# Two 14-megabyte streams of weights on another DMA queue, a conversion step in another order, and the second part's sums formed inside the last group of the first

## The chip, the cores and the metric

The kernel runs on one core of a Trainium2 chip. Its time is the device time of one execution, in microseconds (us). TensorE (PE in the profile) multiplies, VectorE (DVE), ScalarE (ACT) and GpSimd (POOL) do elementwise work, and SyncE (SP) issues nearly all DMAs of the kernel before. A DMA is an instruction in an engine's own stream: it stands in order between that engine's other instructions, waits there for its own condition, and what is behind it waits with it.

## What is computed

Three independent results in fp32, all of them from one launch:

```python
# attention: B, H, S, D = 4, 8, 576, 64, with a memory read mixed in
# moe:  x (2304, 512), w_in (512, 2048), w_out (2048, 512)
h = x @ w_in
g = np.maximum(0.01 * h, h)
moe = g @ w_out
# moe2: x (2304, 512), w_a and w_b (512, 1536), w_out (1536, 512)
a = x @ w_a
b = x @ w_b
moe2 = a * b @ w_out
```

Attention is untouched by the change and ends near 195 us. What follows is about moe and moe2.

## The kernel before, in words

**Every operand is a pair.** An fp32 matrix is held as a high and a low copy of a type that TensorE takes at full rate, and one product is three matmuls (`three`, lines 393 to 396: L394 and L395 need the high copy of the moving operand, L396 its low copy). A high copy is a cast, usually on ACT (L1064, L1326, L1177); the low copy is a subtraction on DVE or POOL one slot later (L1065, L1328, L1182).

**moe** goes over the 2304 tokens in part 0 (1024 tokens) and part 1 (1280), and over eight groups of 256 hidden columns. `inward` makes a group's hidden values: matmuls with `w`, the leaky ReLU on ACT (L1100, into `gf`), the cast on ACT (L1064, into tiles called `qs`, `hl`, `xs`, `g`) and the subtraction (L1065). `outward` multiplies them with `w_out` and adds to `xf` on DVE (L1118). Group 0 is done first for both parts (195 to 241 us); then part 0 runs the sets of groups [1,2], [3,4], [5,6], [7] (241 to 397 us), and part 1 runs [1,2] (397 to 461), [3,4] (461 to 523), [5] (523 to 566) and [6,7] (566 to 622).

**The weights are converted while this runs.** Raw weights come as pairs of 32-bit words (L178, `wraw`). An item of 128x512 is converted in four quarters, one after another on DVE: `one` (L292, L293), `two` (L304, L305), `three_` (L311), `four`; ACT makes the absolute value that an item begins with, here called the sign step (`absolute`, L261, into `wh`), and the high copy (`high`, L299 for moe's own weights into `w`, L301 for the last items into `wr`). Before, the quarter `two` of item n also issues `high` of n and the sign step of item n+1. There are three kinds of items: moe's own (`four` is L316 and L317), 24 "plain" ones of w_a and w_b (`four` is L324) and 12 "last" ones of moe2's w_out (`four` is L334 and L335). `convert(w, rate)` after each slot issues quarters in proportion to the slot's width. The scratch tiles `wh`, `wa`, `wr` exist twice, so item n+2 writes over those of item n.

**Where weights go.** A finished group of moe is written to `kept` in DRAM (L320, 14 times 1 MB) and read again for part 1 (L367, 14 times 1 MB). Plain items go to `plain` (L331), last items to `saved` (L337 from `wr`, L338 from `wh`). All of these are issued by SP, in the order of the program, and so is the next `wraw`.

**moe2** uses a seven-product scheme for w_a and w_b. It needs sums of the token matrix (S1 to S4, made by DVE at L1173, cast by L1178 or L1177, low copies by L1184 on DVE or L1182 on POOL) and sums of the weights (`Matrices.make`, one of 12 pairs after another). In pr 0 it runs over the tokens of part 0 (622 to about 808 us), in pr 1 over the rest. A block q is a string of products, by their digits, and of output slots O, which multiply the last finished a*b (tiles `hl`, `qs`; cast L1326, low copy L1328) with w_out: before, the string of an odd q is `1O6O5OO7234`, that of an even one `1657O2O3O4O`. Products are taken out of PSUM by L1343 and joined by L1370, all on DVE, as the slots of O are (L1405). At the end of pr 0 come the O slots of the last group, O(5,0) first, and there, from the slot (O, 5, 2) on, before forms the second part's sums, with two jobs per slot, while its last outputs run.

**What sets the order.** Code is written in the order of the slots; `after(k, fn)` puts a piece of work k slots later and `tick` runs what is due. An engine then executes its own instructions strictly in that order. There is no dynamic scheduling.

Of the kernel before, what the change touches and what calls it, by code (L numbers as in the profile page):

```python
# [117 lines left out]
def attention_moe_moe2(ctx: ExitStack, tc, kqT, qn, vn, m_prev, beta, w_in, w_out, w_a, w_b, w_o2, out):  # L118
# [38 lines left out]
    class Weights:  # L157


        def __init__(self, first, ab, last):  # L160
# [6 lines left out]
            self.plain = [dram.tile([P, 4, 2 * P], F32, tag=f"plain{m}", name=f"plain{m}") for m in range(12)]  # L167
# [116 lines left out]
        def quarters(self, n, item):  # L284
# [29 lines left out]
            def four():  # L314
                if kind == "own":
                    V.tensor_tensor(t["a"], t["a"], f32(self.tiles[i][:, 0, c]), ALU.subtract)  # L316
                    V.tensor_tensor(self.tiles[i][:, 1, c], t["a"], t["h"], ALU.add)  # L317
                    if part:
                        w = f32(self.tiles[i]).rearrange("p s c -> p (s c)")
                        nc.sync.dma_start(self.kept[i], w)  # L320
                    self.done.add(item)
                elif kind == "plain":
# [6 lines left out]
                    v = t["r"].rearrange("p (f c) -> p f c", f=2)  # L329
                    for f in range(2):  # L330
                        nc.sync.dma_start(self.plain[i][:, (0, 3, 1, 2)[part * 2 + f]], v[:, f])  # L331
                    self.done.add(item)
                else:
                    V.tensor_tensor(t["a"], t["a"], t["r"], ALU.subtract)  # L334
                    V.tensor_tensor(t["h"].bitcast(F32R), t["a"], t["h"], ALU.add)  # L335
# [795 lines left out]
    class Sums:  # L1131
# [27 lines left out]
        def jobs(self, y, raw):  # L1159
# [9 lines left out]
            def of(x, k):  # L1169
                return plain(x)[:, k] if x[0] == "A" else raw[(int(x[1]) - 1) * 2 + k]  # L1170
# [9 lines left out]
            def lo(x, eng):  # L1180
# [6 lines left out]
            early = [[hi("A11"), lo("A11", G)]]  # L1187
            middle = [
                [total("S1", "A21", "A22", ALU.add)],
                [total("S2", "S1", "A11", ALU.subtract), hi("S1")],  # L1190
                [hi("S2"), lo("S2", V)],
                [lo("S1", V), total("S4", "A12", "S2", ALU.subtract)],
                [hi("A12"), lo("A12", G), total("S3", "A11", "A21", ALU.subtract)],
                [hi("S3"), lo("S3", V)],
            ]
            end = [[hi("S4"), lo("S4", V)], [hi("A22"), lo("A22", G)]]
# [402 lines left out]
```

## Time and profile before

| | us |
|---|---|
| median of 3 runs | 1049.18 (1048.68 to 1051.09) |
| profiled execution | 1049.15 |
| its span | 1047.4 |
| PE busy | 1007.4 (96%) |
| DVE busy | 797.4 (76%) |
| ACT busy | 416.6 (40%) |
| POOL busy | 337.2 (32%) |

The execution is 1.8 us longer than its span. PE is busy nearly all the time, so that the question is what it loses in which stretch: where it stands still, and where the granted clock is at its lower level afterwards. The views are the table of stretches (busy time of each engine, the granted clock as a share of the full 2.4 GHz), the list of waits, and the instructions in order of time. A matmul's record is longer than the distance to the next one, because matmuls are pipelined.

### The profile page before, as it was taken

What the parts mean: (1) busy time and instruction counts of PE and PEld (TensorE: products, weight loads), DVE (VectorE), ACT (ScalarE), POOL (GpSimd) and SP (SyncE); (2) the same over time, 40 slices, a digit from 0 to 9 for tenths busy, and PEclk for the clock granted to TensorE, in tenths of its full rate; (3) what the DMA queues carried; (4) which work ended last, traced back from release to release, by engine and by line L of the source; (5) the groups of instructions that cost most, each with busy time, mean ns of one, the idle gap of its engine ahead of it and who ended that gap; (6) DMA issues with size and microseconds to landing.
All of it is one profiled execution on the core that took longest, in us unless ns stands there. A gap on an engine that the chain in (4) does not pass through costs nothing.

```text
span 1047.4 us, 14692 instructions
## 1 busy us (share of the span) xinstructions
PE 1007.4 (96%) x5266; PEld 806.4 (77%) x5266; DVE 797.4 (76%) x1555; ACT 416.6 (40%) x935; POOL 337.2 (32%) x324
## 2 busy tenths in 40 slices
PE   9999999989999999899979999999999999999998
PEld 4666667768878787687757888887777788888887
DVE  7999998789999987897976277677777736547546
ACT  7988885655353432315241523421222222101101
POOL 6787767312030311204011545544534100000000
PEclk9999999989999999899988999999999999999999
DMA  8325431255454578665774135666464433333412
GB/s 246 103 103 156 155 102 47 74 207 200 162 200 174 182 249 321 215 219 191 239 241 141 62 132 191 239 241 225 166 250 173 154 142 137 143 139 121 158 44 101
DMA packets 52729, 176.60 MB, mean 169 GB/s; under 512 B 5552, under 2 KB 18608, under 8 KB 42672
## 3 DMA queue, kind: packets, MB, share of 16 engines
q1 hardware_dynamic: 52512, 175.66, 48.2%
q8 instruction: 41, 0.67, 0.3%
q14 instruction: 32, 0.26, 0.1%
q10 hardware_dynamic: 144, 0.00, 0.0%
HBM read 117.44 MB, written 58.20 MB: 168 GB/s over the span
## 4 chain that ended last, share of the span: by engine, by line
PE 55%; DVE 28%; DMA 8%; ACT 4%; issue 3%; POOL 1%; SPq 0%; ACTq 0%; DVEq 0%; POOLq 0%
PE b L396 14%; PE b L394 14%; PE b L395 14%; PE b L745 4%; DVE wa L304 4%; PE b L824 3%; DVE xf L1118 3%; DVE wh L311 3%; DVE wh L292 3%; PE b L686 3%; DMA saved<-wh 2%; DMA wraw<-in_w_a 2%; DVE wh L305 2%; DVE wa L293 2%; DVE w L317 2%
## 5 line engine op out<-in xcount | busy, mean ns | idle before, releaser
L1343 DVE TENSOR_TENSOR gf<-b,gf 128x512 f32<-128x512 f32 x168 | 115.3, 688 | 76.2 <-PE b L396 72.5
L1405 DVE TENSOR_TENSOR xf<-b,xf 128x512 f32<-128x512 f32 (+1 forms) x91 | 62.1, 683 | 63.5 <-PE b L396 63.4
L394 PE MATMUL b<-xh,w 128*128 128x512 f32 x256 | 101.6, 397 | 0.4 <-ACT gf L1100 0.4
L395 PE MATMUL b<-xh,w 128*128 128x512 f32 x256 | 100.2, 391 | 0.0
L396 PE MATMUL b<-xh,w 128*128 128x512 f32 x256 | 99.9, 390 | 0.0
L1065 POOL TENSOR_TENSOR hl<-gf,hl 128x512 fp32r<-128x512 f32 (+1 forms) x26 | 36.7, 1422 | 168.1 <-ACT hl L1064 134.3
L261 ACT ACTIVATE wh<-wraw 128x512 f32<-128x512 f32 x64 | 43.0, 671 | 105.3 <-DMA wraw<-in_w_a 35.3
L395 PE MATMUL b<-xs,bhi 128*128 128x512 f32 (+1 forms) x216 | 79.7, 369 | 1.9 <-DVE xs L1184 1.9
L394 PE MATMUL b<-xs,bhi 128*128 128x512 f32 (+1 forms) x216 | 79.8, 369 | 0.6 <-DVE gf L1343 0.6
L396 PE MATMUL b<-xs,blo 128*128 128x512 f32 (+1 forms) x216 | 79.7, 369 | 0.0
L395 PE MATMUL b<-xs,ahi 128*128 128x512 f32 (+1 forms) x216 | 79.0, 366 | 0.0
L394 PE MATMUL b<-xs,ahi 128*128 128x512 f32 (+1 forms) x216 | 79.0, 366 | 0.0
L396 PE MATMUL b<-xs,alo 128*128 128x512 f32 (+1 forms) x216 | 78.9, 365 | 0.0
L640 ACT ACTIVATE p<-p,stat 128x512 f32<-128x512 f32 (+3 forms) x128 | 71.0, 559 | 4.5 <-DVE stat L694 4.2
L394 PE MATMUL b<-hl,w 128*128 128x512 f32 (+1 forms) x164 | 62.4, 380 | 10.1 <-ACT hl L1064 10.1
L1065 POOL TENSOR_TENSOR qs<-gf,qs 128x512 fp32r<-128x512 f32 (+1 forms) x21 | 30.3, 1451 | 124.2 <-ACT qs L1064 107.9
L667 POOL TENSOR_SCALAR p<-p,stat,keep 128x128 f32<-128x128 f32 (+3 forms) x95 | 61.4, 661 | 15.7 <-DVE stat L655 13.3
L395 PE MATMUL b<-hl,w 128*128 128x512 f32 (+1 forms) x164 | 62.2, 379 | 0.6 <-DVE hl L1065 0.6
L396 PE MATMUL b<-hl,w 128*128 128x512 f32 (+1 forms) x164 | 61.6, 376 | 0.0
L694 DVE CUSTOM_DVE_ANT_0 p<-b,mask 128x512 f32<-128x512 f32 (+3 forms) x128 | 57.6, 478 | 5.4 <-PE b L686 5.0
L1326 ACT CAST hl<-gf 128x512 fp32r<-128x512 f32 (+1 forms) x40 | 23.1, 578 | 96.3 <-DVE gf L1370 92.9
L396 PE MATMUL b<-w,hl 128*128 128x512 f32 (+1 forms) x146 | 57.5, 394 | 2.7 <-POOL hl L1328 1.4
(196 smaller groups left out, 2673.9 us busy)
## 6 DMA issues: line engine op xcount, KB each, us to landing
kept<-w SPq DMA_DIRECT2D x14, 1024.0 KB, 4.8
w<-kept SPq DMA_DIRECT2D x14, 1024.0 KB, 7.2
w<-saved SPq DMA_DIRECT2D x12, 1024.0 KB, 6.9
wraw<-in_w_in SPq DMA_DIRECT2D x16, 512.0 KB, 3.7
wraw<-in_w_out SPq DMA_DIRECT2D x16, 512.0 KB, 3.6
qraw<-in_qn SPq DMA_DIRECT2D x8, 768.0 KB, 6.7
wraw<-in_w_b SPq DMA_DIRECT2D x12, 512.0 KB, 4.3
plain<-wr SPq DMA_DIRECT2D x48, 128.0 KB, 4.0
```

The source lines that it names most:

```text
L261: nc.scalar.activation(t["h"], self.raw[n][:, :, 1].bitcast(F32), AF.Abs)
L304: V.scalar_tensor_tensor(u["a"], raw[:, :, 1], 0xC0000000, u["a"], ALU.bitwise_and, ALU.bitwise_or)
L394: nc.tensor.matmul(outp, l_hi, r_hi, start=start, stop=False)
L395: nc.tensor.matmul(outp, l_hi, r_lo, start=False, stop=False)
L396: nc.tensor.matmul(outp, l_lo, r_hi, start=False, stop=stop)
L640: nc.scalar.activation(t, t, AF.Exp, bias=s[:, 0, col : col + 1], scale=-1.0, accum_out=s[:, 1, col : col + 1])
L667: ENG[eng].tensor_scalar(live[p], live[p], stats[w % 3][:, 3, col : col + 1], k, ALU.mult, ALU.mult)
L694: nc.vector.tensor_tensor_reduce(one(p, [P, wd]), plan.tiles[banks[j]][:, c : c + wd], mask[:, off : off + wd], -0.125, BIG, ALU.add, ALU. ...
L745: nc.tensor.transpose(tt[0:kw, n * 128 : n * 128 + 128], live[name][:, kt * 128 : kt * 128 + kw], ident)
L1065: after(1 if eng is nc.vector else 2, lambda: eng.tensor_tensor(t[:, 1, c], gf, f32(t)[:, 0, c], ALU.subtract))
L1343: nc.vector.tensor_tensor(left[q, to], src, left[q, add], ALU.add)
L1405: nc.vector.tensor_tensor(y[:, i, c], op, y[:, i, c], ALU.add)
```

## The change

1. `kept` is written (L320) and read (L367) by DMAs that ACT issues instead of SP, each two slots later than before (`after(2, ...)`). That is 28 DMAs of 1 MB.
2. A plain item is written with one DMA instead of two; the sums of the weights read it through another layout (`PLACE`).
3. `high` of item n moves from quarter `two` to `three_`, the sign step of item n+1 from `two` to `four`. For the last items the second word of the pair is formed in `wa` instead of `wh` and saved from there.
4. The rates of `convert` fall from 0.7 to 0.4 in group 0's outward of part 0 (205 us) and from 0.85 to 0.75 in its inward of part 1.
5. moe2's strings become `16572O3O4OO` for an even q, and `1O65O7234OO` for the last block of pr 0; pr 1 has `16572O3O4OOOOTT`. The first O of a block thus stands one product later.
6. In `Matrices.make` the high and low copies, the next load and the write of the finished matrices are each one slot later.
7. The second part's sums are formed in the last block of pr 0 (q = 11), product by product (`1a`, `b6`, `5`, `cd7`, `2`, `3`, `4`), with their intermediate sums in the raw tile of the weights, and one job per slot.

```diff
-                nc.sync.dma_start(self.saved[i][:, 1, part], t["h"])
+                nc.sync.dma_start(self.saved[i][:, 1, part], t["a"])
...
-                        nc.sync.dma_start(self.kept[i], w)
+                        after(2, lambda: nc.scalar.dma_start(self.kept[i], w))
...
-                nc.sync.dma_start(f32(self.tile(i)).rearrange("p s c -> p (s c)"), self.kept[self.again[i - 18]])
+                t = f32(self.tile(i)).rearrange("p s c -> p (s c)")
+                after(2, lambda t=t, i=i: nc.scalar.dma_start(t, self.kept[self.again[i - 18]]))
...
             def two():
...
+            def three_():
                 high()
+                V.scalar_tensor_tensor(t["h"], self.raw.pop(n)[:, :, 0], 2.0**-52, t["h"], ALU.mult, ALU.mult)
+                self.more(n + 2)
+
+            def four():
                 if n + 1 in self.items:
                     self.absolute(n + 1)
...
-                text = ("1657O2O3O4O", "1O6O5OO7234")[a] if g else "1657234"
+                text = ("16572O3O4OO", "1O65O7234OO" if g == 5 else "1O6O5OO7234")[a] if g else "1657234"
...
-            convert(w, 0.7)
+            convert(w, 0.4)
...
-            convert(w, 0.85)
+            convert(w, 0.75)
...
-            if pr == 0 and (kind, q, k) == ("O", 5, 2):
-                sums.last(y1)
-                jobs += sum(sums.jobs(y1, spares), [])
-            run(2)
+            if (pr, kind, q) == (0, "P", 11):
+                if k == "1":
+                    sums.last(y1)
+                    t = mats.raw
+                    steps = sums.jobs(y1, [t[:, i * 512 : i * 512 + 512] for i in range(4)])
+                jobs += [steps[x] for x in {"1": "1a", "6": "b6", "5": "5", "7": "cd7", "2": "2", "3": "3", "4": "4"}[k]]
+            run(1)
```

Three places show what moves on an engine.

ACT at the beginning of group 0's outward of part 1, about 219 us. `gf <- b` is the ReLU that empties a PSUM bank, `hl0 <- gf` the high copy that PE multiplies next, `w <- wa` and `wh <- wraw` are the conversion's high copy and sign step. Before:

```order
L1100 ACTIVATE gf0_2860<-b6_2847 128x512
L299 CAST w_2816<-wa_2819 128x512
L261 ACTIVATE wh_2867<-wraw_2823 128x512
L1064 CAST hl0_2844<-gf0_2860 128x512
L1100 ACTIVATE gf1_2887<-b0_2874 128x512
```

and with the change:

```order
L1099 ACTIVATE gf0_2844<-b6_2831 128x512
L320 DMA kept2_74<-w_2754 128x2048
L1063 CAST hl0_2828<-gf0_2844 128x512
L1099 ACTIVATE gf1_2867<-b0_2854 128x512
L299 CAST w_2869<-wa_2823 128x512
L261 ACTIVATE wh_2874<-wraw_2803 128x512
```

The two conversion steps now stand behind the copy `hl0` and the next ReLU, and a write of `kept` stands in front of that copy.

SP in the first set of part 1, about 402 us: raw weights (`wraw`), kept groups (`w`) and plain items. Before:

```order
L178 DMA wraw_4375<-in_w_b 128x1024
L367 DMA w_4377<-kept4_76 128x2048
L367 DMA w_4379<-kept5_77 128x2048
L367 DMA w_4381<-kept6_78 128x2048
L331 DMA plain3_91<-wr_4318 128x256 x2
L178 DMA wraw_4440<-in_w_a 128x1024
L331 DMA plain4_92<-wr_4364 128x256 x2
```

and ACT there with the change:

```order
L261 ACTIVATE wh_4385<-wraw_4306 128x512
L366 DMA w_4350<-kept4_76 128x2048
L366 DMA w_4351<-kept5_77 128x2048
L366 DMA w_4352<-kept6_78 128x2048
L1063 CAST qs0_4366<-gf1_4380 128x512
L1099 ACTIVATE gf2_4410<-b6_4397 128x512
```

The three reads have left SP's queue, where raw weights stood behind them, and stand on ACT ahead of a copy that PE needs.

DVE in the last block of pr 0. `gf <- b` takes a product out of PSUM, `gf <- gf` joins products, `xf <- b` adds an O slot, `hl0` is the low copy of a*b that O(5,0) needs. Before, after the last product:

```order
L1370 TENSOR_TENSOR gf_6020<-gf_6016,gf_6020 128x512
L1328 TENSOR_TENSOR hl0_7454<-gf_6021,hl0_7454 128x512
L1405 TENSOR_TENSOR xf_6416<-b3_7494,xf_6416 128x512
L1405 TENSOR_TENSOR xf_6416<-b4_7504,xf_6416 128x512
L1405 TENSOR_TENSOR xf_6416<-b5_7513,xf_6416 128x512
L1173 TENSOR_TENSOR gf_6015<-xf_2923 128x512
```

and with the change (`raw` holds the sums, `xs` their low copies):

```order
L1172 TENSOR_TENSOR raw_4353<-xf_2900,raw_4353 128x512 x2
L1347 TENSOR_TENSOR gf_5989<-b1_7432,gf_5989 128x512
L1374 TENSOR_TENSOR gf_5993<-gf_5989,gf_5993 128x512
L1172 TENSOR_TENSOR raw_4353<-xf_2900 128x512 x2
L1347 TENSOR_TENSOR gf_5991<-b2_7446,gf_5991 128x512
L1374 TENSOR_TENSOR gf_5995<-gf_5991,gf_5995 128x512
L1183 TENSOR_TENSOR xs2_5997<-raw_4353,xs2_5997 128x512 x2
L1347 TENSOR_TENSOR gf_5990<-b6_7461,gf_5990 128x512
L1374 TENSOR_TENSOR gf_5994<-gf_5990,gf_5994 128x512
L1332 TENSOR_TENSOR hl0_7428<-gf_5995,hl0_7428 128x512
```

Sums and their low copies that stood behind the first O slots of the last group now stand between the products, ahead of `hl0`.

## Rows read from the trace of the kernel before

**Rows 1.** Stretches: us, then busy of PE, PEld, DVE, ACT, POOL; granted clock, DMA share, GB/s.

```profile
220.00:241.00 21.00, 16.59 (x72) 13.13 (x71) 17.50 (x30) 11.54 (x25) 1.69 (x2) 0.84 0.63 244
241.00:397.00 156.00, 153.39 (x674) 125.68 (x673) 145.34 (x227) 61.23 (x108) 31.94 (x20) 1.00 0.56 196
397.00:461.00 64.00, 57.96 (x288) 48.72 (x287) 53.87 (x88) 18.42 (x35) 12.25 (x9) 0.95 0.69 238
461.00:523.00 62.00, 57.09 (x294) 48.16 (x293) 52.19 (x86) 22.23 (x41) 12.27 (x9) 1.00 0.69 228
523.00:566.00 43.00, 34.07 (x145) 27.26 (x144) 34.76 (x61) 13.02 (x24) 3.99 (x3) 0.86 0.64 217
706.00:778.00 72.00, 70.00 (x307) 56.93 (x306) 56.07 (x82) 16.87 (x31) 37.20 (x27) 1.00 0.52 195
778.00:831.00 53.00, 48.97 (x209) 39.03 (x208) 35.84 (x51) 13.39 (x21) 15.54 (x7) 0.94 0.56 202
```

**Rows 2.** PE in time order around the wait at 428.5: start, length, line.

```profile
428.28 0.39 PE L395 MATMUL b<-hl,w 128*128 128x512 f32 x1
428.51 0.39 PE L396 MATMUL b<-hl,w 128*128 128x512 f32 x1
433.31 0.80 PE L394 MATMUL b<-hl,w 128*128 128x512 f32 x1 [4.42 <-ACT hl L1064]
```

**Rows 3.** Waits over the span: who waited for whom, us in total, times, longest.

```profile
PE b L394 <- ACT hl L1064: 10.1, 3, 4.4
PE b L394 <- ACT xs L1064: 5.3, 1, 5.3
...
PE b L396 <- POOL hl L1328: 1.4, 1, 1.4
PE b L396 <- DVE hl L1328: 1.3, 2, 0.7
```

**Rows 4.** ACT in time order, 222 us: a high copy, with the wait before it.

```profile
222.73 0.62 ACT L299 CAST w<-wa 128x512 fp32r<-128x512 f32 x1 [2.61 <-DVE wa L304]
```

**Rows 5.** SP's DMA issues in time order, 402 to 406 us: start, length of issue.

```profile
402.02 1.33 SPq L367 DMA_DIRECT2D w<-kept  x3
...
406.01 0.33 SPq L178 DMA_DIRECT2D wraw<-in_w_a  x1
```

**Rows 6.** ACT's sign steps in time order, 416 to 428 us.

```profile
416.52 0.66 ACT L261 ACTIVATE wh<-wraw 128x512 f32<-128x512 f32 x1 [8.78 <-DMA wraw<-in_w_a]
...
427.15 0.67 ACT L261 ACTIVATE wh<-wraw 128x512 f32<-128x512 f32 x1 [5.52 <-DMA wraw<-in_w_b]
```

**Rows 7.** ACT in time order, 543 us: a sign step, with the wait before it.

```profile
543.03 0.66 ACT L261 ACTIVATE wh<-wraw 128x512 f32<-128x512 f32 x1 [4.11 <-DMA saved<-wh]
```

**Rows 8.** DVE in time order: two steps of a last item, 553 us.

```profile
553.33 0.69 DVE L304 SCALAR_TENSOR_TENSOR wa<-wraw,wa 128x512 uint32<-128x512 uint32 x1
554.06 0.43 DVE L305 TENSOR_SCALAR wh<-wa 128x512 uint32<-128x512 uint32 x1
```

**Rows 9.** DMA issues: line, engine, KB each, median us from issue to landing.

```profile
w<-kept SPq DMA_DIRECT2D x14, 1024.0 KB, 7.2
...
saved<-wh SPq DMA_DIRECT2D x12, 256.0 KB, 4.5
```

**Rows 10.** POOL in time order, 798 to 811 us.

```profile
798.55 2.38 POOL L1157 TENSOR_TENSOR xs<-xf,xs 128x1024 fp32r<-128x1024 f32 x1
...
807.92 2.39 POOL L1182 TENSOR_TENSOR xs<-xf,xs 128x1024 fp32r<-128x1024 f32 x1 [4.64 <-ACT xs L1177]
```

**Rows 11.** DVE in time order, 798 to 812 us: an O slot, then sums.

```profile
798.05 0.69 DVE L1405 TENSOR_TENSOR xf<-b,xf 128x512 f32<-128x512 f32 x1 [0.88 <-PE b L396]
...
804.96 1.27 DVE L1173 TENSOR_TENSOR gf<-gf,xf 128x512 f32<-128x512 f32 x2
...
808.13 3.33 DVE L1173 TENSOR_TENSOR gf<-xf,gf 128x512 f32<-128x512 f32 x2
```

**Rows 12.** Waits on DVE: who waited for whom, us in total, times, longest.

```profile
DVE wh L292 <- ACT wh L261: 15.1, 13, 4.4
```

More of the change, by code (lines that the diff above doesn't have):

```diff
@@ L166, in __init__ @@
             self.kept = [dram.tile([P, 4 * WC], F32, tag=f"kept{i}", name=f"kept{i}") for i in range(16)]
-            self.plain = [dram.tile([P, 4, 2 * P], F32, tag=f"plain{m}", name=f"plain{m}") for m in range(12)]
+            self.plain = [dram.tile([P, 2, WC], F32, tag=f"plain{m}", name=f"plain{m}") for m in range(12)]
             self.saved = [dram.tile([P, 2, 2, WC], F32, tag=f"saved{g}", name=f"saved{g}") for g in range(6)]
@@ L314, in four @@
             def four():
+                if n + 1 in self.items:
+                    self.absolute(n + 1)
                 if kind == "own":
@@ L327, in four @@
                     )
-                    v = t["r"].rearrange("p (f c) -> p f c", f=2)
-                    for f in range(2):
-                        nc.sync.dma_start(self.plain[i][:, (0, 3, 1, 2)[part * 2 + f]], v[:, f])
+                    nc.sync.dma_start(self.plain[i][:, part], t["r"])
                     self.done.add(item)
@@ L1169, in of @@
             def of(x, k):
-                return plain(x)[:, k] if x[0] == "A" else raw[(int(x[1]) - 1) * 2 + k]
+                return plain(x)[:, k] if x[0] == "A" else raw[((int(x[1]) - 1) * 2 + k) % len(raw)]
             def total(x, a, b, op):
@@ L1185, in lo @@
                 return lambda: after(1, fn)
[L1187 to L1196, printed above, removed]
-            return [[lambda fns=fns: [fn() for fn in fns] for fns in x] for x in (early, middle, end)]
+            steps = {
+                "1": [hi("A11"), lo("A11", G)],
+                "a": [total("S1", "A21", "A22", ALU.add)],
+                "b": [total("S2", "S1", "A11", ALU.subtract)],
+                "6": [hi("S2"), lo("S2", V)],
+                "5": [hi("S1"), lo("S1", V)],
+                "c": [total("S4", "A12", "S2", ALU.subtract)],
+                "d": [total("S3", "A11", "A21", ALU.subtract)],
+                "7": [hi("S3"), lo("S3", V)],
+                "2": [hi("A12"), lo("A12", G)],
+                "3": [hi("S4"), lo("S4", V)],
+                "4": [hi("A22"), lo("A22", G)],
+            }
+            return {k: lambda fns=fns: [fn() for fn in fns] for k, fns in steps.items()}
     class Matrices:
-        PLACE = {"B11": 0, "T1": 1, "B21": 2, "T2": 3, "B22": 4, "T3": 5, "B12": 6, "T4": 7}
+        PLACE = {"B11": 0, "T1": 1, "B12": 2, "T2": 3, "B21": 4, "T3": 5, "B22": 6, "T4": 7}
         def __init__(self, raw):
@@ L1234, in load @@
             weights.until("plain", m)
-            self.when = now[0]
-            nc.sync.dma_start(self.raw.rearrange("p (b t c) -> p b t c", b=4, t=2)[:, :, 0], weights.plain[m])
+            nc.sync.dma_start(
+                self.raw.rearrange("p (b t c) -> p b t c", b=4, t=2)[:, :, 0], weights.plain[m].rearrange("p h (f c) -> p (h f) c", f=2)
+            )
         def make(self, m):
@@ L1244, in make @@
             k = max(0, self.when + 5 - now[0])
+            self.when = now[0] + k + 6
             def total(o, a, b):
@@ L1264, in make @@
             for p in range(4):
-                after(k + p, hi(p))
-                after(k + 1 + p, low(p))
+                after(k + 1 + p, hi(p))
+                after(k + 2 + p, low(p))
             if m < 11:
-                after(k + 5, lambda: self.load(m + 1))
-            after(k + 6, keep)
+                after(k + 6, lambda: self.load(m + 1))
+            after(k + 7, keep)
         def fetch(self, m):
@@ L1493, in attention_moe_moe2 @@
                 mats.load(0)
+                mats.when = now[0]
             if (kind, g) == ("u", 7) and n == 1:
                 n = 2
-                jobs += sums.jobs(y0, None)[0]
+                jobs.append(sums.jobs(y0, None)["1"])
                 mats.make(0)
@@ L1509, in attention_moe_moe2 @@
                 sums.second()
-                early, middle, end = sums.jobs(y0, spares)
-                jobs += middle
+                steps = sums.jobs(y0, spares)
+                jobs += [steps[k] for k in "ab65c2d7"]
                 mats.make(1)
@@ L1515, in attention_moe_moe2 @@
         run(len(jobs))
-        jobs += end
+        jobs += [steps[k] for k in "34"]
         gtags.pop()
         for pr, (kind, q, k) in moe2(ps, sums, mats, spares):
-            if pr == 0 and (kind, q, k) == ("O", 5, 2):
-                sums.last(y1)
-                jobs += sum(sums.jobs(y1, spares), [])
-            run(2)
+            if (pr, kind, q) == (0, "P", 11):
[5 more added lines that the diff above has]
+            run(1)
         while tasks:
```

7 lines of the change are left out of this document (2 added, 5 removed).

## Prediction

> **What bounds the kernel now.** I read the table of stretches first [rows 1]. What a stretch of PE loses there is its length less PE's busy time, plus its length times what the granted clock lacks. 523 to 566 us: 43 - 34.07 = 8.9, and 43 x 0.14 = 6.0, together 15.0. The clock has two levels here, so a mean of 0.86 over 43 us is 12 us at the lower one (1.2 GHz); that spell comes behind the stretch's waits. The same sum gives 7.8 for 220 to 241, 2.6 for 241 to 397, 9.2 for 397 to 461, 4.9 for 461 to 523, 2.0 for 706 to 778 and 7.2 for 778 to 831: 48.7 in all. This is somewhat low, since a record is 0.39 long while the next matmul starts after 0.23: a wait hides its first 0.16. At 428.51 the row says 4.42, while the next matmul starts 4.80 later, that is 4.57 late [rows 2]. Start-to-start distances of all matmuls of these stretches (71, 671, 286, 291, 144, 305 and 207 of them) give 7.7, 3.9, 9.1, 6.4, 15.8, 2.9 and 8.6, together 54.4. These I use. Before 195 us nothing changes, and after 831 us almost nothing is lost.
>
> Next, who is waited for [rows 3]: the two heaviest groups are ACT's high copies at L1064 (10.1 in 3 waits, 5.3 in one). ACT has little to do, so these copies are late because ACT stands at something else, and the time order shows at what: at 222 us at a conversion copy that waits for DVE [rows 4], at 416 and 427 us at sign steps that wait for raw weights [rows 6], at 543 us at a sign step whose scratch is still being saved [rows 7]. The bound is thus PE, interrupted by ACT's queue; behind it DVE, which is busy 145.3 of 156 us in part 0 and nearly as much later.
>
> **The change, part by part.** The profiled run took 1049.15 with a span of 1047.4; 1.8 lie outside and stay. It stands at the median of 1049.18, so I add to the one what I would add to the other.
>
> *220 to 241 us.* ACT stood 2.61 at a conversion copy [rows 4] in front of the copy that PE wanted. That conversion copy now stands behind it, and the lower rates leave DVE with less queued. The stall and its clock spell go: 7.7 becomes 0.5. In front of the same copy now stands a write of `kept`; if that waits as long as the conversion copy did, 4 of the 7.7 stays. Gain 7.2 (3.7 to 7.7).
>
> *Queue and rates in part 0, 241 to 397.* The lower rates take 8 slots x 512 x 0.00266 x 0.3 = 3.3 quarters, and 5120 x 0.00266 x 0.1 = 1.4, from group 0: 4.6 quarters, 4.7 us of DVE, which must be done later. DVE has 10.7 us of room in this part, but the rates here are unchanged, so the work moves on to the end, to group [5]. The sign step moves half an item later, which costs DVE a wait where ACT is not ahead. 3.9 becomes 2.3; gain 1.6 (-1 to 3).
>
> *[1,2], 397 to 461.* Three reads of `kept`, 3 MB, were issued at 402.02, ahead of raw weights issued at 406.01 [rows 5], for which the sign step waited until 416.52 [rows 6]: 10.5 us, where a read of even 1 MB lands in 7.2 as a rule [rows 9]. DVE starved, asked late for the next raw item, and the second wait of 5.52 at 427.15 followed. With `kept` on ACT's queue, two slots later, raw weights stand in no queue behind it. 28 issues of 0.33 to 0.44 (1.33 for three) [rows 5] put 9 to 12 us on ACT over 350 us in which it is at most half busy; they are hidden by that, unless one waits. 9.1 becomes 2.5; gain 6.6 (3 to 9).
>
> What this trace shows is that raw weights behind 3 MB took 10.5 us. The Trainium skill ("DMA: Bandwidth & Descriptors", section "Issuing engines are not separate DMA queues") says that DMAs from several engines run on the same 16 DMA engines and interleave, so that issuing from another one saves only issue time. It speaks against this edit; whether a small transfer gets past a large one when they interleave is what no run here shows. Taken strictly, that rule is the second rival below.
>
> *[3,4], 461 to 523.* Here the waits are shorter and for DVE as much as for ACT; the later sign step takes away the ACT part. 6.4 becomes 1.5; gain 4.9 (3 to 6).
>
> *[5], 523 to 566.* A last item costs DVE four operations of 0.69 and three of 0.43 [rows 8], 4.05. The sign step used to wait until `wh` was saved (4.11 at 543 [rows 7]). It now waits for nothing there; instead `wa` is what is saved, and the next user of that tile comes two quarters later and on DVE. But DVE has 34.8 us of work in this stretch [rows 1], and 4.7 more that group 0 left over: 39.5, where PE needs 27.2 (120 matmuls of 512 columns' worth at 0.227). The difference is 12.3, of which some 3.3 can hang over at the end while PE works from other banks. So 15.8 becomes 9: the wait changes from ACT's queue to DVE's work. Lower end 5 (DVE no longer held up by the waits for ACT, and 2 us of operations that stretched), upper end 14 (`wa` not yet saved: it lands in 4.5 [rows 9], an item takes 4.05, so up to 0.5 and an issue's time for each item). Gain 6.8 (1.8 to 10.8).
>
> *First O of a block one product later, 706 to 778.* The low copy of a*b was late by 0.7 at three blocks (0.7 and 0.6 for the two on DVE and 1.4 for the later one on POOL [rows 3]). One product more ahead is 6 x 0.227 = 1.4: the stalls go. 2.9 becomes 0.4; gain 2.5 (2 to 2.9). The later steps in `Matrices.make` are hidden by the time of a block; the halved count of `plain` DMAs is off the path, SP being no bound. Both at 0.
>
> *The last block of pr 0 and the end of pr 0, 778 to 831.* Here I expect a loss. Low copies and sums of the second part now stand between the products. Counted from the block's start, PE needs 11 slots of 1.36 until O(5,0), which is at 15.0. DVE has, from the first sum to the low copy `hl0`, seven pairs at 1.28 [rows 11] and 13 operations at 0.69: 9.0 + 9.0 = 18.0 us. When does the first sum begin? It is due at about 4.1, but two low copies on POOL (2.38 and 2.39 [rows 10]) begin a little later and end at about 9.1, and this trace shows that a DVE operation that reads two SBUF tensors does not proceed beside a POOL one: the pair at 808.13 took 3.33 beside the POOL operation of 807.92 to 810.31, where another pair took 1.27 [rows 10, 11]. So the first sum ends its wait at 9.1, `hl0` comes at 9.1 + 18.0 + 1.7 (one more such block) = 28.8, less 0.45 for two matmuls that need only the high copy: O(5,0) is 13.3 late, and with a clock spell of 1.7 that is 15. The stalls of this stretch of today (8.6, a part of them behind the sums themselves at the beginning of pr 1) are replaced by it, since the sums are ready before pr 1. 8.6 becomes 15; loss 6.4. Bounds: without any contention `hl0` comes at 4.1 + 18.0 = 22.1, O(5,0) is 6.7 late, with a spell 8 (gain 0.6); a longer block of POOL gives 20 (loss 11.4).
>
> The sum: 7.2 + 1.6 + 6.6 + 4.9 + 6.8 + 2.5 - 6.4 = 23.2, and 0.5 of the stretch after [5]: 23.7. 1049.15 - 23.7 = 1025.
>
> **Rivals.**
> (a) *The sums don't collide.* DVE takes the first sum before POOL starts, so the last block is at its bound of 8, and [5] ends at 6. For it: a wait of 5 us on POOL is my replay, no row. Against: DVE's 18.0 us stand in order whatever POOL does. 1025 - 7 - 3 = 1015.
> (b) *Another queue is no other path.* The raw weights come as late as now, as the 16 engines are full (DMA share 0.69 over the stretch [rows 1]). Then [1,2] keeps its 9.1: 1025 + 6.6 = 1032. Against it: the waiting item is 0.5 MB behind 3, in one queue.
> (c) *The wait only changes its engine.* The change doesn't do what it says for the last items and the sums: DVE waits for the saving of `wa` as ACT did, [5] stays at 14, and the last block costs 20: 1025 + 5 + 5 = 1035.
> (d) *Slower: DVE waits for the sign step.* It now comes a quarter, not three, ahead of its user at L292. Today this wait is 15.1 in 13 times, 1.16 each [rows 12]. There are 57 items between 241 and 566. If one whole sign step (0.66 [rows 7]) is exposed for each, that is 38, less DVE's 10.7 of room in part 0: 27, more than the gain of 24, so 1052. It decides from (24 + 10.7) / 57 = 0.6 per item. Against it: while DVE runs behind PE, ACT is ahead of it and the wait vanishes by itself.
>
> **How the numbers follow.** The forecast 1025 (its own range 1017 to 1034) has a chance of 0.46, (a) 0.20, (b) 0.12, (c) 0.10, (d) 0.12. The range leaves out (d): it goes from 1009 (every term at its good end, 1049 - 40) to 1042 (the bad ends of [5] and the last block and (b) together give 1025 + 5 + 5 + 7). Within 0.2% (2.1 us, about what a measurement of this kernel can tell from no change) needs (c) or (d) to just balance the gains: 0.05. Slower by more is most of (d): 0.10. Faster 0.85.
>
> **What would show it.** Right: no wait of PE on `hl` near 220, 428 and none on `xs` at 538; sign steps of the first set of part 1 that wait under 4 us for raw weights; in [5] PE's waits name DVE at L1118 and DVE is busy without gaps; a new wait of PE on the low copy (L1328 now) of 10 us or more at the end of pr 0, behind DVE pairs that take 2.5 to 3.5; no wait at the beginning of pr 1. Wrong: waits of ACT at its DMA issues, gaps of DVE before L292 at each item, or a last block without a wait.

## The result, and the profile after

| | before | after |
|---|---|---|
| median, us | 1049.12 (4 runs) | 1036.23 (1034.33 to 1036.27, 4 runs) |
| ratio to before | | 0.9869, 95% interval 0.9852 to 0.9886 |
| span of the profiled execution | 1047.4 | 1034.5 |

The kernel is faster by 12.9 us. 23.7 had been forecast; the time lies in the range of 1009 to 1042, outside the forecast's own 1017 to 1034, and the gain is a little over half. In one experiment, the conversion's order alone, two of four executions took 2246 and 3504 us; its ratio is formed from the other two. The table of stretches of the kernel after, with its edges at the same matmuls as in [rows 1] (columns as there; the edges to a tenth):

```profile
220.20:234.60 14.40, 14.07 (x74) 11.95 (x73) 12.21 (x24) 9.24 (x20) 0.00 (x0) 1.00 0.76 255
234.60:391.50 156.90, 153.86 (x673) 125.67 (x672) 148.45 (x233) 62.58 (x109) 31.29 (x20) 1.00 0.57 202
391.50:450.90 59.40, 57.05 (x288) 48.40 (x287) 52.01 (x85) 18.59 (x35) 12.09 (x9) 0.97 0.71 245
450.90:508.70 57.80, 56.39 (x292) 47.94 (x292) 52.48 (x84) 21.22 (x40) 11.91 (x9) 1.00 0.74 241
508.70:548.70 40.00, 31.71 (x146) 25.84 (x145) 34.96 (x63) 13.83 (x26) 3.70 (x3) 0.90 0.73 252
548.70:604.80 56.10, 56.10 (x289) 48.24 (x288) 31.21 (x47) 22.42 (x41) 26.63 (x19) 0.98 0.21 76
688.70:757.80 69.10, 69.10 (x306) 57.26 (x305) 52.10 (x83) 18.28 (x32) 35.79 (x26) 1.00 0.53 193
757.80:818.20 60.40, 50.79 (x208) 40.50 (x207) 39.69 (x52) 13.02 (x21) 14.41 (x7) 0.89 0.55 196
```

Set against [rows 1]:

| stretch | before | after | gain | forecast |
|---|---|---|---|---|
| group 0, outward of part 1 | 21.0 | 14.4 | 6.6 | 7.2 |
| part 0 | 156.0 | 156.9 | -0.9 | 1.6 |
| [1,2] | 64.0 | 59.4 | 4.6 | 6.6 |
| [3,4] | 62.0 | 57.8 | 4.2 | 4.9 |
| [5] | 43.0 | 40.0 | 3.0 | 6.8 |
| [6,7] | 56.0 | 56.1 | -0.1 | 0.5 |
| first O later | 72.0 | 69.1 | 2.9 | 2.5 |
| last block and end of pr 0 | 53.0 | 60.4 | -7.4 | -6.4 |

The gains add up to 12.9, the whole difference of the spans. Who PE waits for now (columns as in [rows 3]):

```profile
PE b L393 <- ACT xs L1063: 5.7, 1, 5.7
PE b L393 <- DVE gf L1347: 4.5, 1, 4.5
PE b L395 <- DVE hl L1332: 3.7, 1, 3.7
PE b L393 <- DVE xf L1117: 3.4, 4, 1.6
PE b L394 <- DVE hl L1064: 3.3, 3, 2.3
```

Line numbers after are one to four off: L1063 is the cast of L1064 before, L1347 the step that takes a product out of PSUM. The waits for `hl` copies on ACT, 10.1 before, are gone. The one for `xs` in [5] (5.3 before) still stands there with 5.7. Three waits of over 2 us are new: 4.5 and 3.7, both in the last block of pr 0, and 2.3 for a low copy on DVE in [1,2] (the longest of the three in the last line).

**The wait in [5].** DMA issues in time order, then ACT's sign step (start, length, and the wait before it):

```profile
514.21 0.33 ACTq L366 DMA_DIRECT2D w<-kept  x1
514.58 0.44 ACTq L366 DMA_DIRECT2D w<-kept  x1
514.65 0.33 SPq L178 DMA_DIRECT2D wraw<-in_w_o  x1
...
523.71 0.66 ACT L261 ACTIVATE wh<-wraw 128x512 f32<-128x512 f32 x1 [4.66 <-DMA wraw<-in_w_o]
...
527.67 0.62 ACT L301 CAST wr<-wa 128x512 fp32r<-128x512 f32 x1 [1.58 <-DVE wa L304]
528.20 0.61 ACT L1063 CAST xs<-gf 128x512 fp32r<-128x512 f32 x1
```

The raw load was issued 0.07 us behind two reads of `kept` that stand in another queue, and landed after 9.0 us (DMA issues of 514.6 to 514.7, last column us to landing):

```profile
wraw<-in_w_o SPq DMA_DIRECT2D x1, 512.0 KB, 9.0
```

The copy that PE needs, `xs` at 528.20, stands behind that sign step on ACT, and then behind a high copy of the conversion that waited another 1.58 for DVE. While the sign step waited, DVE ran out of work:

```profile
520.23 0.69 DVE L333 TENSOR_TENSOR wa<-wa,wh 128x512 fp32r<-128x512 f32 x1
524.41 0.43 DVE L292 TENSOR_SCALAR wh<-wh 128x512 f32<-128x512 f32 x1 [3.49 <-ACT wh L261]
525.47 1.04 DVE L293 TENSOR_SCALAR wa<-wh 128x512 uint32<-128x512 uint32 x1 [0.64 <-DMA saved<-wa]
```

**The last block of pr 0.** DVE's first pair of sums:

```profile
761.80 5.44 DVE L1172 TENSOR_TENSOR raw<-xf 128x512 f32<-128x512 f32 x2
```

The two sums of that pair, one by one:

```profile
761.80 2.64 DVE L1172 TENSOR_TENSOR raw<-xf 128x512 f32<-128x512 f32 x1
764.37 2.88 DVE L1172 TENSOR_TENSOR raw<-xf 128x512 f32<-128x512 f32 x1
```

And POOL in time order:

```profile
761.50 2.40 POOL L1156 TENSOR_TENSOR xs<-xf,xs 128x1024 fp32r<-128x1024 f32 x1 [6.04 <-ACT xs L1155]
763.85 2.84 POOL L1181 TENSOR_TENSOR xs<-xf,xs 128x1024 fp32r<-128x1024 f32 x1
```

A pair of sums that takes 1.27 alone [rows 11] took 5.44. Its first sum ended at 764.44, half a us after POOL's first copy, its second at 767.25, half a us after the second copy: each sum was held by one copy. The two long waits of PE that follow are for product 4's bank and for the low copy of O(5,0):

```profile
774.03 0.79 PE L393 MATMUL b<-xs,ahi 128*128 128x512 f32 x1 [4.47 <-DVE gf L1347]
...
787.74 0.80 PE L395 MATMUL b<-w,hl 128*128 128x512 f32 x1 [3.69 <-DVE hl L1332]
```

### The profile page after: what moved, and what is told of

The parts are those of the page before. It is cut to its first block, busy times and chain, and to the rows that moved or that the text cites. A ratio compares the mean times of both kernels' runs of the same rounds, so it can differ in the third digit from the quotient of the medians.

```text
span 1034.5 us, 14605 instructions
## 1 busy us (share of the span) xinstructions
PE 1001.9 (97%) x5266; PEld 804.9 (78%) x5266; DVE 797.0 (77%) x1555; ACT 417.1 (40%) x935; POOL 331.8 (32%) x324
## 4 chain that ended last, share of the span: by engine, by line
PE 66%; DVE 22%; DMA 6%; issue 2%; ACT 2%; POOL 1%; SPq 0%; ACTq 0%; DVEq 0%
PE b L394 18%; PE b L393 18%; PE b L395 18%; PE b L744 4%; PE b L823 3%; DVE wa L304 3%; DMA wraw<-in_w_b 3%; DVE wh L309 3%; PE b L685 3%; DVE wh L292 2%; DVE wa L293 2%; DVE xf L1117 2%; DVE wh L305 2%; DVE w L317 1%; DMA saved<-wa 1%
## 5 line engine op out<-in xcount | busy, mean ns | idle before, releaser
L1347 DVE TENSOR_TENSOR gf<-b,gf 128x512 f32<-128x512 f32 x168 | 114.9, 689 | 77.9 <-PE b L395 72.3
L1064 POOL TENSOR_TENSOR hl<-gf,hl 128x512 fp32r<-128x512 f32 (+1 forms) x26 | 36.3, 1405 | 158.7 <-ACT hl L1063 98.3
L1064 POOL TENSOR_TENSOR qs<-gf,qs 128x512 fp32r<-128x512 f32 (+1 forms) x21 | 28.8, 1384 | 119.7 <-ACT qs L1063 90.5
L394 PE MATMUL b<-hl,w 128*128 128x512 f32 (+1 forms) x164 | 61.3, 374 | 3.3 <-DVE hl L1064 3.3
L1099 ACT ACTIVATE gf<-b 128x512 f32<-128x512 f32 (+1 forms) x76 | 41.9, 551 | 55.6 <-PE b L395 54.6
L393 PE MATMUL b<-hl,w 128*128 128x512 f32 (+1 forms) x164 | 61.4, 374 | 0.0
L395 PE MATMUL b<-hl,w 128*128 128x512 f32 (+1 forms) x164 | 61.1, 372 | 0.0
```

Source lines behind the costliest of these rows:

```text
L393: nc.tensor.matmul(outp, l_hi, r_hi, start=start, stop=False)
L394: nc.tensor.matmul(outp, l_hi, r_lo, start=False, stop=False)
L395: nc.tensor.matmul(outp, l_lo, r_hi, start=False, stop=stop)
L1064: after(1 if eng is nc.vector else 2, lambda: eng.tensor_tensor(t[:, 1, c], gf, f32(t)[:, 0, c], ALU.subtract))
L1099: nc.scalar.activation(gf, hp[:, 0:n], AF.Prelu, alpha=0.01)
L1347: nc.vector.tensor_tensor(left[q, to], src, left[q, add], ALU.add)
```

## Experiments

Stretches are named as in the table above, and "the changed kernel" is the one after. Ratios are to the kernel before, run on the same chip.

**Kept on SP's queue again.**

```diff
-                        after(2, lambda: nc.scalar.dma_start(self.kept[i], w))
+                        after(2, lambda: nc.sync.dma_start(self.kept[i], w))
...
-                after(2, lambda t=t, i=i: nc.scalar.dma_start(t, self.kept[self.again[i - 18]]))
+                after(2, lambda t=t, i=i: nc.sync.dma_start(t, self.kept[self.again[i - 18]]))
```

> The changed kernel with one part undone: writes and reads of kept are issued by SP again (still two slots late). Theory A, as in the prediction: a queue of its own lets raw weights pass the reads of kept; undone, ACT's sign steps in the first set of part 1 wait 9 us again, the 6.6 us of that term come back: 1043 us. Theory B, formed from the trace of the changed kernel, where a raw load issued beside two reads of kept landed after 9.0 us and one without them after 4.3: transfers share the engines whichever queue they stand in, and the queue is worth nothing: 1036 within 3 us.

Ratio 0.9851 (0.9832 to 0.9870), median 1033.84: not slower; from the changed kernel it can't be told apart. A queue of its own is not needed for the gain in [1,2], which is 58.9 here. [3,4] loses 2.5 against the changed kernel and [5] gains 3.3:

```profile
392.60:451.50 58.90, 56.70 (x287) 48.27 (x286) 49.90 (x80) 18.57 (x35) 11.96 (x9) 0.97 0.67 243
451.50:511.80 60.30, 56.83 (x294) 48.09 (x293) 54.14 (x88) 21.46 (x40) 12.17 (x9) 1.00 0.71 239
511.80:548.50 36.70, 29.81 (x146) 23.52 (x144) 34.94 (x61) 13.55 (x26) 4.17 (x3) 1.00 0.80 270
```

The raw loads show how the two differ. Beside the three reads at the beginning of [1,2], the two raw loads took 3.8 and 9.1 us here (DMA issues of this kernel in two short windows, last column us to landing):

```profile
wraw<-in_w_b SPq DMA_DIRECT2D x1, 512.0 KB, 3.8
...
wraw<-in_w_b SPq DMA_DIRECT2D x1, 512.0 KB, 9.1
```

and 8.1 and 9.4 in the changed kernel:

```profile
wraw<-in_w_b SPq DMA_DIRECT2D x1, 512.0 KB, 8.1
...
wraw<-in_w_b SPq DMA_DIRECT2D x1, 512.0 KB, 9.4
```

In one queue the load that is issued 1.1 us ahead of the reads is undisturbed and the one behind waits for them; in two queues, where the first load is issued 0.2 us behind one read and 0.2 ahead of the other two, both are slow.

**Kept on ACT's queue, nothing else.** The kernel before with the change's first point.

```diff
-                        nc.sync.dma_start(self.kept[i], w)
+                        after(2, lambda: nc.scalar.dma_start(self.kept[i], w))
...
-                nc.sync.dma_start(f32(self.tile(i)).rearrange("p s c -> p (s c)"), self.kept[self.again[i - 18]])
+                t = f32(self.tile(i)).rearrange("p s c -> p (s c)")
+                after(2, lambda t=t, i=i: nc.scalar.dma_start(t, self.kept[self.again[i - 18]]))
```

> The kernel before with one part of the change alone: kept written and read on ACT's queue, two slots later. Theory A, as in the prediction: raw weights no longer stand behind reads of kept, the waits at 416 and 427 us go: 1043 us. Theory B, from the run with kept on SP's queue, which lost nothing: the engines are shared, nothing is gained, and ACT may stand at an issue now and then: 1049 us within 3, or more.

Ratio 1.0004 (0.9984 to 1.0025): nothing in the sum. Group 0, part 0, [1,2] and [5]:

```profile
220.30:242.70 22.40, 17.01 (x72) 13.40 (x71) 17.66 (x31) 11.83 (x26) 1.68 (x2) 0.85 0.66 244
242.70:405.40 162.70, 157.17 (x673) 127.91 (x672) 148.90 (x232) 61.01 (x107) 30.95 (x20) 0.98 0.55 194
405.40:465.00 59.60, 57.06 (x288) 48.37 (x287) 50.83 (x83) 18.49 (x36) 11.17 (x9) 0.97 0.67 238
525.50:566.20 40.70, 32.31 (x145) 25.41 (x144) 34.24 (x59) 13.32 (x24) 4.36 (x3) 0.92 0.66 229
```

[1,2] and [5] gain 4.4 and 2.3, group 0 and part 0 lose 1.4 and 6.7. From 380 us to the end of part 0 PE is busy for 22.3 of 25.4 us, at a granted clock of 0.93. There, where a read is issued at 381.36 and a raw load 0.9 us later, ACT's sign step waits, and a copy for PE stands behind it:

```profile
390.34 0.66 ACT L261 ACTIVATE wh<-wraw 128x512 f32<-128x512 f32 x1 [5.74 <-DMA wraw<-in_w_b]
```

That raw load landed after 8.0 us. So the wait moved, from behind the reads in one queue to beside them in two.

**The conversion's order, nothing else.**

```diff
             def two():
...
-                high()
-                if n + 1 in self.items:
-                    self.absolute(n + 1)
...
             def three_():
+                high()
...
             def four():
+                if n + 1 in self.items:
+                    self.absolute(n + 1)
...
-                    V.tensor_tensor(t["h"].bitcast(F32R), t["a"], t["h"], ALU.add)
+                    V.tensor_tensor(t["a"].bitcast(F32R), t["a"], t["h"], ALU.add)
...
-                    nc.sync.dma_start(self.saved[i][:, 1, part], t["h"])
+                    nc.sync.dma_start(self.saved[i][:, 1, part], t["a"])
```

> The kernel before with one part of the change alone: high in quarter three_, the sign step in quarter four, the last items' second word formed and saved in wa. Theory A: this order is what frees ACT's queue: the waits of PE for high copies near 220, 428 and 538 us shrink, by 4, 5 and 4 us, with some more in [3,4]: 1034 to 1038 us. Theory B, the slower rival of the prediction: the sign step comes too late for its user L292, DVE waits for it item by item and the gain is eaten: 1046 us or more.

Ratio 0.9861 (0.9827 to 0.9894, two executions), span of its profile 1034.9: this one edit gives as much as the whole change, though not in the same places. Group 0, [1,2], [3,4] and [5] (against 21.0, 64.0, 62.0 and 43.0 before):

```profile
220.40:239.20 18.80, 14.31 (x73) 11.69 (x72) 15.87 (x30) 10.42 (x22) 0.91 (x1) 1.00 0.70 266
394.50:454.60 60.10, 56.79 (x288) 48.21 (x287) 51.45 (x84) 18.72 (x35) 12.11 (x9) 0.97 0.69 241
454.60:516.60 62.00, 57.88 (x294) 49.03 (x293) 54.97 (x90) 22.06 (x42) 11.71 (x9) 0.97 0.71 236
516.60:554.30 37.70, 30.94 (x145) 25.10 (x144) 33.91 (x59) 12.96 (x24) 3.94 (x3) 0.91 0.74 247
```

[3,4] gains nothing from it. The slower rival, DVE waiting for the late sign step, did not come: that wait is 15.2 us in 12 times here and 16.8 in 10 in the changed kernel, where it was 15.1 in 13 [rows 12].

**The rates undone.**

```diff
-            convert(w, 0.4)
+            convert(w, 0.7)
...
-            convert(w, 0.75)
+            convert(w, 0.85)
```

> The changed kernel with one part undone: the rates of group 0 are 0.7 and 0.85 again. Theory A, as in the prediction: the lower rates moved 4.6 quarters of conversion, 4.7 us of DVE, into group [5], which DVE bounds; undone, [5] takes 36 us instead of 40 and a wait near 220 us comes back for 2 to 4 us: 1035 us. Theory B: [5] is held up by a raw load (9.0 us to land beside two reads of kept) and not by DVE's amount of work; [5] stays at 40 and only the wait near 220 comes back: 1039 us.

Ratio 0.9866 (0.9839 to 0.9892), the same time as the changed kernel, by theory A's sum: group 0 takes 18.5 (4.1 more), [5] 37.1 (2.9 less).

```profile
221.40:239.90 18.50, 15.84 (x72) 12.79 (x71) 15.81 (x30) 10.79 (x22) 0.88 (x1) 0.91 0.78 283
513.70:550.80 37.10, 31.44 (x145) 25.70 (x144) 33.57 (x59) 13.21 (x24) 3.90 (x3) 0.91 0.71 252
```

What was saved near 220 us is given back later, but only a small part of it is DVE work in [5]: DVE is busy there for 33.6 us here and for 35.0 in the changed kernel. Most of the moved work runs in [6,7] (this run, then the kernel before; in the changed kernel DVE has 31.2 there):

```profile
550.80:605.90 55.10, 55.10 (x289) 47.53 (x288) 25.91 (x41) 22.02 (x40) 26.26 (x19) 1.00 0.19 67
```

```profile
566.00:622.00 56.00, 56.00 (x290) 48.15 (x290) 26.85 (x39) 22.22 (x40) 26.83 (x19) 0.98 0.18 63
```

And [5] still has a wait of over 4 us at the same copy. There DVE stood behind the saving of `wa`, and ACT behind DVE:

```profile
529.41 0.43 DVE L293 TENSOR_SCALAR wa<-wh 128x512 uint32<-128x512 uint32 x1 [2.71 <-DMA saved<-wa]
```

**The sums after pr 0's last block, as before.** The jobs are queued from (O, 5, 2) on, two per slot, and the string of the last block is `1O6O5OO7234`.

```diff
-            if (pr, kind, q) == (0, "P", 11):
...
-            run(1)
+            if pr == 0 and (kind, q, k) == ("O", 5, 2):
+                sums.last(y1)
+                steps = sums.jobs(y1, spares)
+                jobs += [lambda ks=ks: [steps[x]() for x in ks] for ks in ("1", "a", "b", "6", "5c", "2d", "7", "3", "4")]
+            run(2)
```

> The changed kernel with one part undone: the second part's sums are formed from the slot (O, 5, 2) on, two jobs per slot, and the last block of pr 0 has the string 1O6O5OO7234 again. Theory A: the sums in the last block cause the whole loss of that stretch (60.4 us instead of 53.0), and undone it is 53 again: 1029 us. Theory B: the loss comes from the later steps in making the weights' sums and the later first O, which stay: 1036 us.

Ratio 0.9822 (0.9797 to 0.9847), median 1031.15. The end of pr 0 takes 55.2, so that 5.2 of the 7.4 lost are back and theory A holds for the greater part; what costs the other 2.2 was not traced:

```profile
760.20:815.40 55.20, 49.19 (x208) 38.82 (x207) 38.21 (x51) 13.20 (x21) 14.64 (x7) 0.94 0.59 216
```

**POOL's two copies later.**

```diff
-            after(1, lambda: nc.gpsimd.tensor_tensor(self.tail[:, 1], y[:, :, e], f32(self.tail)[:, 0], ALU.subtract))
+            after(12, lambda: nc.gpsimd.tensor_tensor(self.tail[:, 1], y[:, :, e], f32(self.tail)[:, 0], ALU.subtract))
...
-                return lambda: after(1, fn)
+                return lambda: after(late if x == "A11" else 1, fn)
...
-                    steps = sums.jobs(y1, [t[:, i * 512 : i * 512 + 512] for i in range(4)])
+                    steps = sums.jobs(y1, [t[:, i * 512 : i * 512 + 512] for i in range(4)], 10)
```

> The changed kernel, with the two low copies that POOL makes at the start of the last block (A11 and the last 256 tokens) 10 and 12 slots later; the work of every engine stays as it is. Theory A: DVE's first sum stands still because POOL runs (a pair of 5.44 us where 1.28 is usual); then it takes about 1.3, the stall of 4.6 us before the product 4 goes, and O(5,0) comes some 4 us sooner: 1032 us or less. Theory B: what holds is the amount of DVE work put in front of the low copy that O(5,0) needs; O(5,0) is late by the same: 1035 to 1036 us.

Ratio 0.9839 (0.9821 to 0.9857), median 1032.29. DVE's first pair of sums:

```profile
761.80 1.28 DVE L1172 TENSOR_TENSOR raw<-xf 128x512 f32<-128x512 f32 x2
```

The same pair, at the same time after the start, takes 1.28 instead of 5.44, and the wait for product 4's bank falls from 4.5 to 0.6. But POOL then runs later, in front of the last copies for O(5,0) (POOL, then what PE waits for):

```profile
778.59 5.10 POOL L1181 TENSOR_TENSOR xs<-xf,xs 128x1024 fp32r<-128x1024 f32 x2 [2.23 <-ACT xs L1176]
783.65 1.73 POOL L1332 TENSOR_TENSOR hl<-gf,hl 128x512 fp32r<-128x512 f32 x1
```

```profile
PE b L395 <- DVE hl L1332: 5.9, 1, 5.9
```

The stretch takes 56.8: of the 4.2 that DVE stood, 3.6 are gained. That POOL holds DVE is shown, and also that this isn't all.

**Two sums early, the rest with the O slots.**

```diff
-            if (pr, kind, q) == (0, "P", 11):
...
+            if (pr, kind, q) == (0, "P", 11) and k == "6":
+                t = mats.raw
+                steps = sums.jobs(y1, [t[:, i * 512 : i * 512 + 512] for i in range(4)])
+                jobs += [steps[x] for x in "ab"]
+            if (pr, kind, q, k) == (0, "O", 5, 0):
+                sums.last(y1)
+                jobs += [steps[x] for x in "165d72c34"]
             run(1)
```

The low copy of the last 256 tokens also comes ten slots late.

> The changed kernel, with only the sums S1 and S2 in the last block; their copies, the other sums and the low copies on POOL are made one job per slot from O(5,0) on. Theory A: both stalls at the end of pr 0 (4.6 and 5.6 us, with their clock spells) are DVE work and POOL's hold in front of the last a*b; both go: 1036 - 11 = 1025 us. Theory B: the work is only moved into the O slots, where DVE then has 1.97 us per slot of 1.36, and a stall of like size stands at the start of pr 1: 1033 us or more.

Ratio 0.9751 (0.9731 to 0.9771), median 1022.73. The end of pr 0 takes 47.3 us, 13.1 less, at the full clock:

```profile
756.90:804.20 47.30, 45.47 (x209) 36.98 (x208) 34.59 (x51) 13.02 (x21) 14.27 (x7) 1.00 0.69 251
```

No wait of over 1 us came at the start of pr 1 in its place: theory A, and a little more than it asked.

**On top of it, the reads of kept six slots late instead of two.**

```diff
-                after(2, lambda t=t, i=i: nc.scalar.dma_start(t, self.kept[self.again[i - 18]]))
+                after(6, lambda t=t, i=i: nc.scalar.dma_start(t, self.kept[self.again[i - 18]]))
```

> The kernel with two sums early (1022.7 us), with the reads of kept six slots late instead of two. Theory A: the stall of 6 us in [5] is a raw load that shares the engines with two reads of kept (9.0 us to land instead of 4.3); with the reads later it lands in 4 to 5 and the stall is under 2: 1018 us. Theory B: the raw load is late because it is asked for late (DVE frees its scratch late), and the stall stays, or PE waits for a kept weight: 1022 us or more.

Ratio 0.9770 (0.9742 to 0.9799), median 1026.22, no gain. [5] falls to 38.3, while [1,2] and [3,4] rise to 61.9 and 62.0. The first two raw loads of [5] now land in 4.4 and 4.3 us and the wait for `xs` falls to 2.0, as theory A says. But the reads meet other raw loads, four of which take 8.6 to 9.9 us; later is not away.

**On top of two sums early, kept on SP's queue**, with the edit shown first.

> The kernel with two sums early (1022.7 us), with kept written and read by SP again, two slots late. Theory A: on a queue of its own a read of kept slows both raw loads around it (8.1 and 9.4 us, 9.0 and 6.9), on SP's queue only the one behind it (3.8 and 9.1, 4.4 and 7.3); so group [5] takes 37 us instead of 40, and the time is 1020 us. Theory B: ACT's and SP's queues are alike in the end, since [3,4] loses what [5] gains: 1022 to 1024 us.

Ratio 0.9715 (0.9690 to 0.9740), median 1020.63. [5] takes 38.0 and not 37. That the queue on ACT costs a little is likely from the two pairs of runs, but neither pair is clear by its intervals.

**The same, with each read in four pieces.**

```diff
-                after(2, lambda t=t, i=i: nc.sync.dma_start(t, self.kept[self.again[i - 18]]))
+                for j in range(4):
+                    c = slice(j * 512, j * 512 + 512)
+                    after(1 + j, lambda t=t, i=i, c=c: nc.sync.dma_start(t[:, c], self.kept[self.again[i - 18]][:, c]))
```

> The kernel with two sums early, with kept on SP's queue and each read of 1 MB cut into four of 256 KB, one per slot. Theory A: what makes raw loads late is the megabytes in front of them at once; with a piece per slot every raw load lands in 4 to 6 us, the stalls near 425 and 520 us shrink under 2 us each, and the time is 1015 to 1018 us. Theory B: what is left in these stretches is DVE's own work; the loads land sooner and the time stays at 1020 to 1023 us.

Ratio 0.9703 (0.9679 to 0.9727), median 1019.24: not clearly faster than in whole reads, so theory B by the time. In its profile the 26 raw loads from 393 to 523 land in 3.3 to 6.8 us (mean 4.7), where whole reads on the same queue gave 3.2 to 7.9 (25 loads, mean 4.8), and [1,2] has nearly no loss left. The profile is of the fastest of five executions (1015.92), 3.3 us under the median, so that a part of this may be chance:

```profile
391.10:446.70 55.60, 55.18 (x288) 47.23 (x287) 49.66 (x78) 19.08 (x35) 11.68 (x9) 1.00 0.76 259
446.70:505.50 58.80, 56.63 (x293) 47.96 (x292) 54.66 (x89) 21.24 (x40) 12.25 (x9) 1.00 0.78 246
505.50:541.80 36.30, 30.89 (x146) 24.81 (x146) 34.48 (x61) 13.73 (x26) 3.64 (x3) 0.95 0.84 277
```

**The same, with the rates undone.**

```diff
-            convert(w, 0.4)
+            convert(w, 0.7)
...
-            convert(w, 0.75)
+            convert(w, 0.85)
```

> The kernel with kept in pieces (1019 us, group [5] 36.3 us, 27.5 of it matmuls), with the rates of group 0 at 0.7 and 0.85 again. Theory A: what is left in [5], 8.7 us, is DVE's work, 4.7 of it moved there by the lower rates; undone, [5] takes 32 us, and the wait near 220 us comes back for 4: 1019 us, the same sum. Theory B: [5] is held up by what lands late (raw loads, saved words) and not by the amount of DVE work; it stays at 36, and the time is 1023 us.

Ratio 0.9696 (0.9671 to 0.9720), median 1018.04, about the same sum again. Between the same matmuls group 0 takes 4.3 more, [1,2] 5.0 more, [3,4] 3.3 less, and [5] only 0.9 less, not 4. The two profiles differ by 3.5 us where the medians differ by 1.2 the other way, so that [1,2] and [3,4] can't be compared to a few us; group 0 comes out as in the first run with the old rates, [5] with less. So theory A has the sum and not the place. This kernel and the one above it have the lowest medians: some 30 us under the kernel before the change, and 17 to 18 under the changed one.

## Why the prediction was right, and where it was not

**Group 0 (7.2, measured 6.6) and the first O (2.5, measured 2.9)** went as worked out. In group 0 two edits do it together: the order alone gives 2.2 (18.8), the order and the rest without the rates 2.5 (18.5), and the rates the remaining 4.1. The write of `kept` in front of that copy costs nothing that shows. For the first O, every run with the new strings takes 69.1 us between these matmuls and every run with the old ones 72.1 (the later steps of `Matrices.make` came with the strings, and no run parts the two); the three late copies there were 0.7, 0.6 and 0.7, all on DVE, and the 1.4 on POOL that the prediction counts with them lies behind 778 us.

**[3,4] (4.9, measured 4.2)** has the right size, but not by the step named for it, "the later sign step takes away the ACT part". With the order alone [3,4] takes 62.0, as before, and PE still waits 3.6 for a copy on ACT there; with the order and all else but the queue it takes 60.3. What gained the 4.2 is not shown, and the agreement is luck.

**Part 0 (1.6, measured -0.9)** lies inside its bounds. The later sign step is not what costs: with the order alone part 0 takes 155.3. What makes 156.9 of it is not shown.

**[1,2] (6.6, measured 4.6).** The size was two thirds right and the reason wrong. The step that failed is what follows from "with `kept` on ACT's queue, raw weights stand in no queue behind it". They stand in none, and land late all the same: after 8.1 and 9.4 us beside the reads, against 10.4 before, and sign steps there still wait 4.0 to 4.4. The queue alone does bring [1,2] to 59.6, but the wait comes back at the end of part 0 and the sum gains nothing; undoing the queue leaves [1,2] at 58.9, and the conversion's order alone brings it to 60.1. Either edit alone shortens PE's waits there, from 6.0 to 2.5 and 3.3 us, and together they give little more than one. Rival (b), another queue is no other path, was right that the raw weights come late. Its reason was not (the engines' share was 0.69, not full), nor its price, since it took the queue to be all that gains there. The rule cited with it agrees with these runs: the Trainium skill ("DMA: Bandwidth & Descriptors", section "Issuing engines are not separate DMA queues") says that DMAs interleave whichever engine issues them, and here 8.1 and 9.4 us stand against 3.8 and 9.1.

**[5] (6.8, measured 3.0)** is the largest miss, and two steps failed. The first is "the wait changes from ACT's queue to DVE's work". PE's longest wait still names ACT's copy `xs`, for 5.7 us, and begins while DVE, held to be the bound, stands still for 3.5; waits for DVE's `xf` come to 2.6. Sign step, raw load and DVE form a ring through ACT: before, the sign step waited for the saving of `wh`; after, for a raw load of 9.0 us beside two reads of `kept`; with the old rates DVE waited 2.7 for the saving of `wa`. The second is "so the work moves on to the end, to group [5]", 39.5 us of DVE in all. DVE is busy for 35.0 there, 34.8 before; most of the moved work runs in [6,7], where DVE has 31.2 against 26.9 before and PE loses next to nothing. With kept on SP's queue [5] is 36.7 and with the reads in pieces 36.3, the 36 that was forecast; there DVE is busy for 34.9 and 34.5 of it and does come near to being the bound. It reaches that length without the 4.7 us that the forecast put in, and undoing the rates took away 0.9.

**The last block (-6.4, measured -7.4)** was worked out from DVE's order and POOL's hold, and both are in the trace: the first pair of sums ended at 767.2, each sum held by one POOL copy, and moving these copies gave 3.6 us, moving most of the sums and their copies 13.1. The low copy `hl0` was forecast for 28.8 us behind the block's start and was done 29.9 behind it. A part of that was not in the forecast: DVE stood 2.0 us at 782 for a cast on ACT. One more detail was off: the delay does not stand at O(5,0) in one piece of 10 us or more, but in two, 4.5 at product 4, whose bank DVE had not emptied, and 3.7 at O(5,0), each with its own clock spell (granted clock 0.89 over the stretch).

**The sum.** The forecast was 10.8 us too good: 3.8 of that in [5], 2.5 in part 0, 2.0 in [1,2], 1.0 in the last block, and 1.5 in small terms. Nearly all misses have the same sign. The terms took a stall that has a visible cause to vanish with it; in [5], and in the run with the queue alone, a part of it came back at the next thing in ACT's queue. For the small terms that is not shown. Rival (c) gave 1035, within 1 us of the measured time, but that is luck: DVE waited for the saving of `wa` for 0.6 us and not as ACT did, and the last block came to 16 and not to 20. In (a) the sums don't collide, and they did; (d) did not come.

## What to carry to other kernels

Don't ask only what an in-order engine waits for, but what stands behind the wait: moving the waiting instruction behind the ones that the critical engine needs was by itself worth as much as this whole change, whose other gains and losses cancel. Giving large transfers another queue does not take them out of the way of small ones, and can slow a small one that in one queue would stand ahead of them. Cutting them into pieces took the longest landing from 7.9 to 6.8 us here, and the time not clearly down. Work that is moved out of a visible stall into a stretch with "room" needs that room on the engine at that place: an estimated 18 us of elementwise work ahead of one needed copy cost more than the stall that it replaced, and with most of it a few slots later nearly nothing was lost.

## What the runs showed of the hardware

- A pair of DVE sums of two SBUF operands took 5.44 us when it began 0.3 us after the first of two POOL copies (2.40 and 2.84), and 1.28 with these copies elsewhere. DVE did get in between the two copies: each sum ended half a us after one of them, and the second copy took 0.44 longer than the first. The Trainium skill ("SBUF — State Buffer", section "SBUF: two separate sides") describes an exclusive lock on a pair of ports that DVE and POOL share, held for the whole instruction by whichever starts first; the trace agrees.
- Of the 28 raw loads of 512 KB of the changed kernel after 390 us, the 13 with a read of `kept` issued up to 6 us ahead of them or up to 2 behind landed in 6.3 us on the mean, the other 15 in 4.0. With the reads on the same queue it was 5.4 (14 loads) and 4.2 (14).
